# Holding MLP units behind attention matmuls in TensorE's order, and pinning the additions of narrow inputs on VectorE

## The chip, the cores and the metric

The kernel runs on one core of one Trainium2 chip. The metric is device time in microseconds (us). Three runs of the kernel before took 1078.59, 1073.54 and 1074.20 us; their median is 1074.2 us. Its profile is of one further execution.

## The reference

Attention over a batch of 4, with 8 heads, 576 positions and a head size of 64, and then two MLPs (512 to 2048 to 512) over all 2304 tokens, one behind the other, all in float32.

```python
scores = scale * np.matmul(q, k.transpose(0, 1, 3, 2))      # (4, 8, 576, 576), scale = 1/8
scores = np.where(causal, -1000000000.0, scores)
a = np.exp(scores - scores.max(-1, keepdims=True))
a /= a.sum(-1, keepdims=True) + 1e-09
local = np.matmul(a, v)
mem_ret = np.einsum('bhsd,bhde->bhse', q_p, M_prev)         # q_p = phi(q), elementwise: elu(q) + 1
mem_norm = np.einsum('bhsd,bhd->bhs', q_p, z_prev)[..., None] + 1e-06
attn_out = g * mem_ret / mem_norm + (1 - g) * local         # g = sigmoid(beta), one number per head

x = attn_out.transpose(0, 2, 1, 3).reshape(2304, 512)
x = elu(x @ moe_w_in) @ moe_w_out                           # first MLP
x = leaky(x @ moe2_w_in) @ moe2_w_out                       # second MLP, leaky(h) = max(0.01 h, h)
```

## The kernel before

**Numbers.** A float32 matrix product is made of products of two halves: each operand is a high part (a rounded copy) and a low part (what the rounding left). xh and xl are the halves of an MLP input, gh and gl those of an activation, dh and dl, ah and al, qph and qpl those of attention's operands. The high part is a copy on ScalarE or VectorE, the low part a subtraction on VectorE or GpSimd. The MLP's three matmuls for each 128 x 128 block of weights are high x high, low weight x high, and high weight x low (`h_mm`, `o_mm`).

**Attention.** A tile is one batch element (`tiles1`, 0 to 3), and in it four pairs of heads are done one after the other. For each head and group of rows there is an item with three stages: its scores (`score`, one or two spans of keys for each block of rows; the score matmuls, lines 428 and 429, go to one of three PSUM banks sc; VectorE reduces them, line 431; ScalarE exponentiates, line 436), its transposes (`t0`, `t1`, `t1b`, `t1c`: GpSimd scales the rows, line 451, TensorE transposes them to a bank tp, line 457, and ScalarE and VectorE split the result into halves, lines 249 and 250), and its products with v and the memory (`pv`, line 524, to the only bank po; VectorE copies po to xp, line 531, which a DMA writes to DRAM). A new pair of heads also needs its keys and queries transposed (lines 294, 339), their halves made (kk, kl, qs; lines 302 and 343), and phi of the queries (lines 330 and 250, qph and qpl, by way of po). `weave` mixes the stages of three items that follow each other.

**MLP units beside attention.** When a tile's attention is done, its 576 tokens go through a part of the first MLP (7 of its 16 blocks of 128 hidden columns) while the next tile's attention runs. `phase1_units` makes the list: for each half of the tile (288 tokens, a narrow input) it loads what attention wrote, adds the two heads' parts (`u_x`, the four additions of line 682, one for each 128 columns, on VectorE; tile 0 has none), splits the sum (`split_x`: line 610 on ScalarE, line 614 on GpSimd), and then come 7 units of 12 matmuls of the first layer (`u_h`, line 621) and 4 units of 21 of the second (`u_o`, line 649). Of tiles 1 to 3 each half's input is read by four DMAs (lines 675 and 676) into x and y, of which there is one buffer each.

**What sets the order.** The loop at lines 762 to 780 goes through attention's units with a planned cost in ns for each. pos is the cost up to here. Once pos has passed the point at which a unit of the MLP may start (its tile's end plus DELAY), each attention unit earns credit, and a unit whose cost is covered is written into the program there. A scheduler then makes each engine's order: it keeps what depends on what, takes what its own timing believes to be ready, and among that goes by priority, by and large the place in the program. `tc.high_priority(offset=FILL_OFF)` lets an MLP unit count as 20 instructions earlier. `tc.keep_in_program_order(add)` forbids that an instruction be moved on its engine past those written around it; before, it stands on the first of each four additions only. On the chip each engine runs its order as it stands and waits at semaphores.

When attention is over, the units left (mostly of tile 3) are merged with the loading of further weights, and the two MLPs' wide stages follow, in which TensorE has a matmul at all times.

Of the kernel before, what the change touches and what calls it, by code (L numbers as in the profile page):

```python
# [19 lines left out]
def _f(ap):  # L20
    return ap.bitcast(F32)
# [3 lines left out]
def kernel(  # L25
# [14 lines left out]
    nc = tc.nc  # L40
# [10 lines left out]
    SHIFT = {"prep": 0.0, "score": -0.3, "tr": 0.0, "pv": -0.1}  # L51
    V32 = 1
    FILL_OFF = 20
    LEAD = 0.4
    PC = 200
    HC = 1.0
# [84 lines left out]
    tiles1 = [(b, 0, 5) for b in range(B)]  # L141
# [64 lines left out]
    def bank(tag):  # L206
        return psum.tile([P, 512], F32, tag=tag, bufs=BANKS[tag], name=tag)
# [31 lines left out]
    def copy(eng, dst, src):  # L239
        if eng == "A":  # L240
            nc.scalar.copy(dst, src)  # L241
        else:
            (nc.vector if eng == "V" else nc.gpsimd).tensor_copy(dst, src)  # L243
# [357 lines left out]
    def mtile(tag, bufs, dt=F32, shape=None):  # L601
        shape = shape or (NW,)
        pool = pools.get(("own", tag), pools["mlp"])
        return pool.tile([P] + list(shape), dt, tag=tag, bufs=bufs, name=tag)

    def split_x(xt, w, par):
        xh = mtile(f"xh{par}", 1, F32R, (NKC, NW))[:, :, 0:w]
        xl = mtile(f"xl{par}", 1, F32R, (NKC, NW))[:, :, 0:w]
        for c in range(NKC):
            hi = nc.scalar.copy(xh[:, c], xt[:, c])  # L610
            if c == 0 and not tail:
                tc.keep_in_program_order(hi)
            pools["cast", par] = hi.ins
            nc.gpsimd.tensor_tensor(out=xl[:, c], in0=xt[:, c], in1=_f(xh[:, c]), op=ALU.subtract)
        return xh, xl

    def h_mm(ph, wi, xh, xl):
        n_mm = 0
        for kc in range(NKC):
            for wj, xx in ((0, xh), (1, xh), (0, xl)):  # L620
                nc.tensor.matmul(ph, wi[:, wj, kc, :], xx[:, kc, :], start=n_mm == 0, stop=n_mm == 11)  # L621
                n_mm += 1
# [8 lines left out]
    def elu(ph, w):  # L631
        e = mtile("e", EB)[:, 0:w]
        nc.scalar.activation(out=e, in_=ph, func=AF.Relu, scale=-1.0)
        nc.scalar.activation(out=e, in_=e, func=AF.Exp, scale=-1.0)
        nc.vector.scalar_tensor_tensor(out=e, in0=e, scalar=-1.0, in1=ph, op0=ALU.add, op1=ALU.max)
        return g_split(e, w)
# [7 lines left out]
    def o_mm(py, fs, key, ec, gs, first, last, opens=True, closes=True):  # L644
        for f in fs:
            wo = wo_tiles[key, f]
            gh, gl = gs[f]
            for n_mm, (wj, gg) in enumerate(((0, gh), (1, gh), (0, gl))):
                nc.tensor.matmul(  # L649
                    py, wo[:, wj, ec * P:(ec + 1) * P], gg,  # L650
                    start=opens and f == first and n_mm == 0, stop=closes and f == last and n_mm == 2,
                )
# [5 lines left out]
    def h_bank():  # L658
        nonlocal n_ph
        n_ph += 1  # L660
        return bank("tp" if tail and n_ph % 2 else "pm")

    def phase1_units(ti):

        mine = [(pi, o, w, {}) for pi, (pt, o, w, _) in enumerate(parts) if pt == ti]

        def u_load(pi, o, w, st):
            xt = st["t"] = mtile("x", 1, F32, (NKC, NW))[:, :, 0:w]
            if ti < V32:
                nc.sync.dma_start(xt, xm_scr[ti][:, :, o:o + w])  # L670
                return
            x2 = st["t2"] = mtile("y", 1, F32, (NKC, NW))[:, :, 0:w]
            for j in range(2):
                ps, pz = slice(64 * j, 64 * j + 64), slice(64 - 64 * j, 128 - 64 * j)
                nc.sync.dma_start(xt[ps], xq_scr[ti][j][ps, :, o:o + w])
                nc.sync.dma_start(x2[ps], xq_scr[ti][j][pz, :, o:o + w])

        def u_x(pi, o, w, st):
            xt = st["t"]
            if ti >= V32:  # L680
                for c in range(NKC):
                    add = nc.vector.tensor_tensor(out=xt[:, c], in0=xt[:, c], in1=st["t2"][:, c], op=ALU.add)
                    if c == 0:
                        tc.keep_in_program_order(add)
            st["x"] = split_x(xt, w, pi % 2)
            for n in range(2):
                nc.sync.dma_start(xp_scr[n][pi], _f(st["x"][n]))
            st["g"] = {}

        units = [(0, lambda: u_x(*mine[0]))]  # L690
        for k, (pi, o, w, st) in enumerate(mine):

            def u_h(f, w=w, st=st):
                ph = h_bank()[:, 0:w]
                h_mm(ph, wi_tiles[0, f], *st["x"])
                st["g"][f] = elu(ph, w)

            def u_o(ec, pi=pi, w=w, st=st):
                py = bank("sc" if tail else "pm")[:, 0:w]
                o_mm(py, range(NFA), 0, ec, st["g"], 0, NFA - 1)  # L700
                y = mtile("st", 2)[:, 0:w]
                copy(E_Y, y, py)
                nc.sync.dma_start(y_scr[pi][:, ec], y)

            for f in range(NFA):
                units.append((HC * 12 * w / 2.4, lambda f=f, u=u_h: u(f)))
                if k + 1 < len(mine) and f == 1:
                    units.append((0, lambda k=k: u_load(*mine[k + 1])))
                if k + 1 < len(mine) and f == NFA - (4 if ti == len(tiles1) - 1 else 2):
                    units.append((0, lambda k=k: u_x(*mine[k + 1])))  # L710
            for ec in range(NKC):
                units.append((3 * NFA * w / 2.4, lambda ec=ec, u=u_o: u(ec)))
        return lambda: u_load(*mine[0]), units

    def merge(a, bu):
# [4 lines left out]
        while ia < len(a) or ib < len(bu):  # L720
            if ib >= len(bu) or (ia < len(a) and fa / ta <= fb / tb + LEAD):
                c, u = a[ia]
# [8 lines left out]
    def close_decode():  # L731
        wst_a.__exit__(None, None, None)
        pools["decode_bank"] = None
        pools["outer"] = tc.tile_pool(name="mlpx", bufs=1, reuse_waits="tile", side="left")
        early = pools["outer"].__enter__()
        for tag in ("x", "y", "xh0", "xl0"):
            pools["own", tag] = early
        pools["own"] = tc.tile_pool(name="mlp", bufs=1, reuse_waits="tile", side="left")
        pools["mlp"] = pools["own"].__enter__()
# [19 lines left out]
    dec = [lambda f=f: load_w(0, wpa, w1i, w1o, f, f) for f in range(NFA)]  # L759
    fill = []  # L760
    credit = pos = 0.0
    for c, u, done in att:
        u()
        pos += c
        while dec and pos >= c0 * DSPAN * (NFA - len(dec)) / NFA:
            with tc.high_priority(offset=0):
                dec.pop(0)()
        if done == 0:
            close_decode()
        if done is not None:  # L770
            fetch, more = phase1_units(done)
            fetch()
            fill += [(pos + DELAY, c2, u2) for c2, u2 in more]
        if fill and fill[0][0] <= pos:
            credit += c * rate
        while fill and fill[0][0] <= pos and fill[0][1] <= credit:
            _, c2, u2 = fill.pop(0)
            credit -= c2
            with tc.high_priority(offset=FILL_OFF):
                u2()  # L780
    side = [(c, u) for _, c, u in fill]
    del pools["cast", 0]
# [117 lines left out]
    for gi, (t0, w) in enumerate(wide):  # L900
        pos = {}
# [61 lines left out]
```

## Time and profile before

| what | value |
|---|---|
| runs | 1078.59, 1073.54, 1074.20 us; median 1074.2 us |
| the profiled execution | 1075.3 us, of which the span of instructions is 1073.5 us |
| TensorE busy | 1042.7 us, 97% of the span |
| VectorE, ScalarE, GpSimd busy | 595.5, 483.5, 532.4 us |
| granted TensorE clock, mean | 0.995 of 2.4 GHz |

The three other engines have most of their work in the first 400 us, beside attention; from there on they wait for TensorE. Times in rows of the trace count from the span's start. PE is TensorE, DVE VectorE, ACT ScalarE, POOL GpSimd. A matmul's own time overlaps the next one's, so what TensorE loses is read from the idle time in square brackets, with what ended it behind the arrow, and not from the times of single matmuls.

### The profile page before, as it was taken

What the parts mean: (1) busy time and instruction counts of PE and PEld (TensorE: products, weight loads), DVE (VectorE), ACT (ScalarE), POOL (GpSimd) and SP (SyncE); (2) the same over time, 40 slices, a digit from 0 to 9 for tenths busy, and PEclk for the clock granted to TensorE, in tenths of its full rate; (3) what the DMA queues carried; (4) which work ended last, traced back from release to release, by engine and by line L of the source; (5) the groups of instructions that cost most, each with busy time, mean ns of one, the idle gap of its engine ahead of it and who ended that gap; (6) DMA issues with size and microseconds to landing.
All of it is one profiled execution on the core that took longest, in us unless ns stands there. A gap on an engine that the chain in (4) does not pass through costs nothing.

```text
span 1073.5 us, 17323 instructions
## 1 busy us (share of the span) xinstructions
PE 1042.7 (97%) x5904; PEld 911.4 (85%) x5904; DVE 595.5 (55%) x1382; ACT 483.5 (45%) x1169; POOL 532.4 (50%) x674
## 2 busy tenths in 40 slices
PE   7998899999998999999999999999999999999997
PEld 4776799989998998988888889888888888888896
DVE  6889987788879748576762325654322221232232
ACT  6999887778877635544442224332211211110111
POOL 7675775667657626654543225855422422222221
PEclk9999999999999999999999999999999999999999
DMA  7754544564446238765562304430200100000010
GB/s 183 197 144 116 162 137 105 124 169 144 108 121 164 89 95 286 251 227 188 191 224 66 118 1 138 157 118 1 79 1 1 64 15 1 10 30 1 1 40 20
DMA packets 150408, 115.05 MB, mean 107 GB/s; under 512 B 80048, under 2 KB 142000, under 8 KB 150320
## 3 DMA queue, kind: packets, MB, share of 16 engines
q1 hardware_dynamic: 150320, 113.94, 35.6%
q8 instruction: 47, 0.77, 0.3%
q14 instruction: 41, 0.34, 0.1%
HBM read 78.52 MB, written 31.85 MB: 103 GB/s over the span
## 4 chain that ended last, share of the span: by engine, by line
PE 87%; DVE 6%; DMA 3%; issue 1%; ACT 1%; SPq 1%; POOL 0%; DVEq 0%; ACTq 0%; POOLq 0%
PE pm L621 20%; PE tp L621 16%; PE sc L911 14%; PE sc L649 10%; PE pm L649 4%; PE po L911 4%; PE po L524 4%; PE tp L457 4%; PE po L649 3%; PE pm L524 2%; PE sc L428 1%; PE sc L426 1%; PE sc L429 1%; DVE pt L431 1%; DMA y<-xq 1%
## 5 line engine op out<-in xcount | busy, mean ns | idle before, releaser
L628 POOL TENSOR_TENSOR gl<-e,gh 128x512 fp32r<-128x512 f32 (+2 forms) x181 | 202.8, 1123 | 378.0 <-DVE gh L243 266.4
L621 PE MATMUL tp<-xw,w 128*128 128x512 f32 (+1 forms) x504 | 144.0, 367 | 0.0
L621 PE MATMUL pm<-xw,w 128*128 128x512 f32 (+1 forms) x496 | 142.1, 369 | 0.0
L911 PE MATMUL sc<-w,gh 128*128 128x512 f32 x448 | 135.9, 390 | 0.0
L451 POOL TENSOR_SCALAR pt<-pt,rs,omg 128x128 f32<-128x128 f32 (+4 forms) x160 | 102.5, 649 | 22.9 <-DVE rs L446 18.2
L649 PE MATMUL sc<-gh,w 128*128 128x512 f32 (+2 forms) x438 | 105.4, 340 | 0.3 <-DVE gh L243 0.3
L621 PEld LDWEIGHTS tp<-xw,w 128*128 128x128 f32 x504 | 91.8, 189 | 16.1
L621 PEld LDWEIGHTS pm<-xw,w 128*128 128x128 f32 x496 | 90.6, 188 | 16.1
L436 ACT ACTIVATE pt<-pt,mx 128x128 f32<-128x128 f32 (+4 forms) x160 | 93.0, 583 | 16.6 <-DVE mx L431 15.7
L911 PEld LDWEIGHTS sc<-w,gh 128*128 128x128 f32 x448 | 83.1, 188 | 16.5
L621 PE MATMUL tp<-xv,w 128*128 128x512 f32 (+1 forms) x252 | 92.5, 367 | 0.0
L621 PE MATMUL pm<-xv,w 128*128 128x512 f32 (+1 forms) x248 | 91.4, 369 | 0.0
L640 ACT ACTIVATE e<-pm 128x512 f32<-128x512 f32 (+1 forms) x40 | 22.2, 554 | 145.2 <-PE pm L621 142.2
L138 POOL TENSOR_TENSOR w<-wm,w 128x512 fp32r<-128x512 f32 x50 | 65.8, 1337 | 37.9 <-ACT w L241 37.9
L641 DVE TENSOR_TENSOR e<-tp,e 128x512 f32<-128x512 f32 (+1 forms) x40 | 25.5, 636 | 106.2 <-ACT e L640 106.2
L911 PE MATMUL sc<-w,gl 128*128 128x512 f32 x224 | 84.3, 389 | 0.0
L243 DVE CAST gh<-e 128x512 fp32r<-128x512 f32 (+2 forms) x146 | 75.4, 520 | 13.8 <-PE po L911 3.1
L649 PEld LDWEIGHTS sc<-gh,w 128*128 128x128 f32 x438 | 74.9, 188 | 9.3 <-DVE gh L243 0.6
L621 PE MATMUL pm<-xh,w 128*128 128x288 f32 x368 | 81.3, 308 | 1.5 <-ACT xh L610 1.4
L457 PE MATMUL tp<-ident,pt 128*128 128x128 f32 x480 | 80.3, 276 | 2.3 <-ACT ah L247 0.8
L641 DVE TENSOR_TENSOR e<-pm,e 128x512 f32<-128x512 f32 (+1 forms) x40 | 25.4, 636 | 102.4 <-ACT e L640 102.4
L640 ACT ACTIVATE e<-tp 128x512 f32<-128x512 f32 (+1 forms) x40 | 22.1, 552 | 117.2 <-PE tp L621 117.2
(157 smaller groups left out, 2444.7 us busy)
## 6 DMA issues: line engine op xcount, KB each, us to landing
wraw<-in_moe_w_in_dram SPq DMA_DIRECT2D x32, 512.0 KB, 3.9
wraw<-in_moe_w_out_dram SPq DMA_DIRECT2D x32, 512.0 KB, 4.7
xh<-xh SPq DMA_DIRECT2D x8, 576.0 KB, 3.1
xl<-xl SPq DMA_DIRECT2D x8, 576.0 KB, 4.1
ys<-st SPq DMA_DIRECT2D x32, 144.0 KB, 2.8
x<-x1s SPq DMA_DIRECT2D x9, 512.0 KB, 3.8
out_dram<-st SPq DMA_DIRECT2D x36, 128.0 KB, 1.7
vn<-in_v_dram SPq DMA_DIRECT2D x64, 64.0 KB, 2.3
```

Of the source, the lines that this page charges most:

```text
L138: nc.gpsimd.tensor_tensor(out=w[:, 1, a], in0=t[:, a], in1=_f(w)[:, 0, a], op=ALU.subtract)
L243: (nc.vector if eng == "V" else nc.gpsimd).tensor_copy(dst, src)
L436: nc.scalar.activation(out=pt[0:m, 0:nk], in_=pt[0:m, 0:nk], func=AF.Exp, scale=-1.0, bias=mx[0:m, last:last + 1], accum_out=self.pd["ss"] ...
L451: nc.gpsimd.tensor_scalar(out=pt, in0=pt, scalar1=rs[0:m, i:i + 1], scalar2=omg[0:m, h:h + 1], op0=ALU.mult, op1=ALU.mult,)
L457: nc.tensor.transpose(dst, self.p[c][:, k0:k0 + kn], ident)
L524: nc.tensor.matmul(po[:, a:b], w, x, start=i == 0, stop=i == len(mms) - 1)
L621: nc.tensor.matmul(ph, wi[:, wj, kc, :], xx[:, kc, :], start=n_mm == 0, stop=n_mm == 11)
L628: nc.gpsimd.tensor_tensor(out=gl, in0=g, in1=_f(gh), op=ALU.subtract)
L640: nc.scalar.mul(t, ph, 0.01)
L641: nc.vector.tensor_tensor(out=t, in0=ph, in1=t, op=ALU.max)
L649: nc.tensor.matmul(py, wo[:, wj, ec * P:(ec + 1) * P], gg, start=opens and f == first and n_mm == 0, stop=closes and f == last and n_mm == 2,)
L911: nc.tensor.matmul(pos[tb], gg[:, tb * P:(tb + 1) * P], wo[:, wj, :], start=f == 0 and n_mm == 0, stop=f == NF - 1 and n_mm == 2,)
```

## The change

Two edits. In `u_x`, every addition of a tile but the last is kept in program order, not only the first of four. In the loop, each attention unit with a cost leaves a mark: the planned position behind it and the last matmul that it traced. Each MLP unit is then traced under `tc.issue_after(hold)`, where hold is the last mark that lies at least SLACK = 4000 planned ns back. That adds an edge, for the order only, from that attention matmul to each instruction of the unit on the same engine, TensorE: in TensorE's order none of the unit's matmuls may stand ahead of it. No wait at run time is added by the edge, no instruction is added or removed, and the other engines' instructions are held by nothing but their data.

```diff
     FILL_OFF = 20
+    SLACK = 4000.0
     LEAD = 0.4
...
                     add = nc.vector.tensor_tensor(out=xt[:, c], in0=xt[:, c], in1=st["t2"][:, c], op=ALU.add)
-                    if c == 0:
+                    if c == 0 or ti < len(tiles1) - 1:
                         tc.keep_in_program_order(add)
...
     credit = pos = 0.0
+    marks = []
+    traced = nc.cur_bb.bb.instructions
+
+    def last_matmul():
+        return next(i for i in reversed(traced) if i.engine == mybir.EngineType.PE)
+
     for c, u, done in att:
         u()
         pos += c
+        if c:
+            marks.append((pos, last_matmul()))
...
             credit -= c2
-            with tc.high_priority(offset=FILL_OFF):
+            hold = next(m for p, m in reversed(marks) if p <= pos - SLACK)
+            with tc.issue_after(hold), tc.high_priority(offset=FILL_OFF):
                 u2()
```

Ten lines are added, so a line of the kernel before stands 1 line further on in most of the changed file (L682 is L683, L621 is L622) and 10 further on behind the loop. TensorE has 935 matmuls of the MLP ahead of its last attention matmul before, and 909 now. The first difference in its order lies at the matmul that starts at 173 us of the trace, the last at 568 us.

TensorE, tile 1, where its second pair of heads is about to begin (kk_3162 and qs_3230 are keys and queries of a head, pt_ are rows of exponentiated scores, gh and gl activations of the MLP). Before:

```order
L524 MATMUL po<-dl_155,vv 128x128
L457 MATMUL tp<-ident,pt_168 128x128
L457 MATMUL tp<-ident,pt_3387 128x128
L428 MATMUL sc<-kk_3162,qs_3230 128x288
L429 MATMUL sc<-kl_1_178,qs_3230 128x288
L457 MATMUL tp<-ident,pt_3394 128x128
```

Now:

```order
L650 MATMUL pm<-gl,w_793 128x288
L429 MATMUL sc<-kk_3162,qs_3230 128x288
L430 MATMUL sc<-kl_1_178,qs_3230 128x288
L650 MATMUL pm<-gh,w_905 128x288 x2
L650 MATMUL pm<-gl,w_905 128x288
L650 MATMUL pm<-gh,w_1010 128x288 x2
L650 MATMUL pm<-gl,w_1010 128x288
L458 MATMUL tp<-ident,pt_3394 128x128
```

The last matmuls of the second layer of tile 0's second half have moved in between attention's: before, the last of them stood 24 rows above the first row shown, and no unit followed until the next tile's input was there.

VectorE, the same place some instructions later (x<-x,y are the additions of the first half of tile 1; qpl, qs_3652 and dl are what the next matmuls of attention need). Before, three of the four additions stand 57 rows further up, and the fourth here:

```order
L431 ISA pt_3585,mx<-sc,mask,mx 128x288
L431 ISA mx 128x1
L682 TENSOR_TENSOR x<-x,y 128x288
L343 TENSOR_TENSOR qs_3652<-sc,qs_3652 64x256
L250 TENSOR_TENSOR dl_147<-tp,dh_145 128x384
```

Now:

```order
L432 ISA pt_3585,mx<-sc,mask,mx 128x288
L432 ISA mx 128x1
L683 TENSOR_TENSOR x<-x,y 128x288 x3
L251 TENSOR_TENSOR ac<-tp,ac 64x320
L683 TENSOR_TENSOR x<-x,y 128x288
L251 TENSOR_TENSOR qpl<-po,qph 128x320
L344 TENSOR_TENSOR qs_3652<-sc,qs_3652 64x256
```

All four additions stand together, ahead of qpl and qs_3652.

VectorE, the additions of the second half of tile 2. Before:

```order
L635 SCALAR_TENSOR_TENSOR e<-e,pm 128x288
L302 TENSOR_TENSOR kl_1_176<-sc,kk_5753 64x256
L682 TENSOR_TENSOR x<-x,y 128x288 x3
L531 COPY xp<-po 128x256
L250 TENSOR_TENSOR dl_155<-tp,dh_153 128x384
```

Now:

```order
L388 SCALAR_TENSOR_TENSOR ph_f<-qn,ph_e 128x640
L447 RECIPROCAL rs<-rs 128x2
L636 SCALAR_TENSOR_TENSOR e<-e,pm 128x288
L683 TENSOR_TENSOR x<-x,y 128x288 x4
L432 ISA pt_5997,mx<-sc,mask,mx 128x288
```

They have moved seven score spans down, and what follows them is the reduction of a score instead of the copy that frees the only bank po.

## Rows read from the trace of the kernel before

**Rows 1.** The page, busy time of each engine (us, share of the span, instructions)
```profile
PE 1042.7 (97%) x5904; PEld 911.4 (85%) x5904; DVE 595.5 (55%) x1382; ACT 483.5 (45%) x1169; POOL 532.4 (50%) x674
```
**Rows 2.** Windows: stretch, length, busy of each engine, clock, DMA share, GB/s
```profile
172.00:394.00 222.00, 214.50 (x1633) 209.81 (x1631) 179.34 (x534) 166.79 (x474) 143.37 (x224) 0.98 0.47 125
394.00:426.00 32.00, 29.69 (x219) 28.93 (x218) 20.62 (x32) 15.07 (x31) 15.68 (x17) 1.00 0.88 282
426.00:1073.50 647.50, 641.60 (x3101) 543.31 (x3099) 250.24 (x389) 160.80 (x273) 254.44 (x219) 1.00 0.24 80
```
**Rows 3.** Waits of PE, 172 to 425 us: total us, times, longest
```profile
PE pm L621 <- ACT xh L610: 1.4, 1, 1.4
PE tp L621 <- DVE e L635: 0.6, 1, 0.6
...
PE tp L457 <- DVE dl L250: 0.4, 2, 0.2
PE sc L649 <- DVE gh L243: 0.3, 1, 0.3
```
**Rows 4.** Timeline of PE: start, us, instruction, [idle before <- what ended it]
```profile
202.47 0.33 PE L428 MATMUL sc<-kk,qs 128*128 128x128 f32 x1 [0.72 <-DVE qs L343]
...
220.19 0.40 PE L428 MATMUL sc<-kk,qs 128*128 128x288 f32 x1 [0.77 <-DVE mx L431]
...
223.81 0.33 PE L428 MATMUL sc<-kk,qs 128*128 128x128 f32 x1 [0.83 <-DVE qs L343]
...
225.44 0.39 PE L524 MATMUL po<-qph,ms 128*128 128x256 f32 x1 [0.43 <-DVE qpl L250]
...
307.75 0.39 PE L428 MATMUL sc<-kk,qs 128*128 128x256 f32 x1 [0.68 <-DVE mx L431]
...
323.21 0.33 PE L428 MATMUL sc<-kk,qs 128*128 128x128 f32 x1 [0.62 <-DVE qs L343]
...
325.86 0.52 PE L330 MATMUL po<-ident,ph_e 128*128 128x128 f32 x3 [0.87 <-DVE qpl L250]
...
344.31 0.41 PE L524 MATMUL po<-qph,ms 128*128 128x320 f32 x1 [1.92 <-DVE xp L531]
```
**Rows 5.** Windows behind two of the idles; the clock is the third number from the right
```profile
226.00:230.00 4.00, 4.00 (x21) 4.00 (x20) 3.87 (x10) 2.02 (x7) 3.19 (x4) 0.57 0.84 321
...
344.00:350.00 6.00, 5.69 (x32) 5.66 (x33) 5.81 (x17) 4.43 (x12) 3.44 (x6) 0.72 0.26 77
```
**Rows 6.** Line 682: count, duration in ns (shortest, middle, longest), first and last start
```profile
L682 DVE TENSOR_TENSOR x<-x,y x24: 445/456/3086, 200.7 to 421.2; 128x288 f32<-128x288 f32 x24
```
**Rows 7.** Timeline of DVE at three groups of additions
```profile
200.68 1.20 DVE L682 TENSOR_TENSOR x<-x,y 128x288 f32<-128x288 f32 x3 [2.02 <-DMA y<-xq]
...
303.36 1.20 DVE L682 TENSOR_TENSOR x<-x,y 128x288 f32<-128x288 f32 x3 [1.38 <-DMA vn<-in_v_dram]
...
339.80 4.12 DVE L682 TENSOR_TENSOR x<-x,y 128x288 f32<-128x288 f32 x3 [1.24 <-DMA xq<-xp]
343.85 0.41 DVE L531 COPY xp<-po 128x256 f32<-128x256 f32 x1
344.18 0.54 DVE L250 TENSOR_TENSOR dl<-tp,dh 128x384 fp32r<-128x384 f32 x1
```
**Rows 8.** Timeline of POOL beside the last of these groups
```profile
341.31 0.80 POOL L628 TENSOR_TENSOR gl<-e,gh 128x288 fp32r<-128x288 f32 x1
342.07 1.53 POOL L614 TENSOR_TENSOR xl<-x,xh 128x288 fp32r<-128x288 f32 x2
```
**Rows 9.** Windows with attention alone on PE (two), and with MLP alone
```profile
214.40:226.60 12.20, 9.85 (x71) 8.22 (x70) 11.38 (x36) 10.93 (x33) 7.65 (x15) 0.99 0.43 113
...
319.30:326.10 6.80, 5.22 (x40) 4.51 (x39) 6.55 (x19) 5.70 (x17) 4.48 (x8) 1.00 0.56 146
...
394.40:404.10 9.70, 9.70 (x75) 9.70 (x75) 2.82 (x6) 1.87 (x5) 2.10 (x4) 1.00 0.69 191
```

## The prediction

> **What bounds the kernel now.** I read the page's busy times first. TensorE is busy for 1042.7 of 1073.5 us [rows 1], so a change can gain only where it idles or runs slowly. The windows by stage [rows 2] say where. After 426 us it is busy for 641.6 of 647.5 us, at full clock; what it idles there lies at the very end, out of reach of an order that is the same from the 568th us on. In 172 to 394 us, attention with MLP units woven in, 7.5 us are missing, and between 394 and 426 us, where attention has ended, 2.3 us. Up to 172 us TensorE's order is unchanged, so what is lost before that stays lost.
>
> The waits [rows 3, 4] name each of these idles. Behind attention they are 0.72 and 0.15 us at 202 us; 0.77, 0.83, 0.24 and 0.43 us between 220 and 226 us; 0.68 us at 307 us; 0.62 and 0.87 us at 323 and 326 us; 1.92 us at 344 us. (The 0.15 and the 0.24 us are the two waits for dl of [rows 3].) That is 7.2 us. After attention come 1.38, 0.32 and 0.61 us, 2.3 us. All of attention's waits are for VectorE. To this the clock is added: from 226 to 230 us, right behind the waits of 220 to 226 us, the granted share is 0.57, and from 344 to 350 us, behind the 1.92 us, 0.72 [rows 5]; TensorE fell from 2.4 to 1.2 GHz each time. It was busy for all or nearly all of both, so this is lost work: 4 x 0.43 = 1.7 us and 6 x 0.28 = 1.7 us. In all 9.5 + 3.4 = 12.9 us can be had, and not more.
>
> Two causes stand behind the waits. The first is the additions of line 682 on VectorE. Three of each four stand early in its order and wait there for their data: 2.02, 1.38 and 1.24 us at 200, 303 and 339 us [rows 7], and the third at 339 us takes 3.09 us where the middle one of 24 takes 0.46 [rows 6], while GpSimd works on without a pause until 343.6 us [rows 8]. The idles at 202, 307 and 344 us follow, each for something that VectorE has behind those additions; the 1.92 us is for the copy at 343.85 us. The second cause is stretches in which TensorE has attention alone. From 214.4 to 226.6 us (68 matmuls in the order) it is busy for 9.85 of 12.2 us, from 319.3 to 326.1 us (39 matmuls) for 5.22 of 6.8 us [rows 9], VectorE being busy for 11.38 and 6.55 us of these. No other run of attention matmuls behind 172 us idles except for the additions; the next longest has 25.
>
> **The pinning.** Now the additions of tiles 1 and 2 stay where the program writes them. In VectorE's order they move back to the need of them: by 12 and 3 score spans in tile 1, by 12 and 7 in tile 2, for the first three of each four. The two first halves need no wait any more, since earlier instructions on VectorE have already waited as far; the second halves wait for DMAs that have had several us more. So the stalls in front of the additions go: at TensorE 0.72 + 0.15 + 0.68 + 1.92 = 3.5 us and, with the last of them, 1.7 us of clock. I take 5.2 us; at least the 0.9 us at 202 us (the plainest case), at most 5.2.
>
> What is late next: the additions now stand as a block in front of other work. In tile 1 these are the subtraction qpl and the copies qs, for which TensorE waits at 223.81 and 225.44 us already [rows 4]; in tile 2 qs, dl and the copy xp. Three additions more, 1.20 us by the first row of [rows 7], stand there each time. In tile 2 I count the 1.2 us whole. Bounds: nothing, if TensorE has enough else to do, and 1.2 + 2.6 = 3.8 us, if one addition waits as the one at 340.84 us did (3.09 - 0.46). At the second halves nothing that TensorE needs at once stands behind the block but a score's reduction, with three PSUM banks between them: 0 us, at most 2.6 us.
>
> The Trainium skill (SBUF — State Buffer, "SBUF: two separate sides") says that a VectorE instruction with two SBUF inputs and a GpSimd instruction that reads SBUF exclude each other, and that the loser waits for the whole instruction of the winner. By that rule a block behind one GpSimd instruction (0.80 us in [rows 8]) would cost 0.8 us; this case's row has 2.6 us across several of them, so the row decides and the upper end above stays.
>
> **The hold.** The units' matmuls can't go ahead of an attention matmul that stands 4000 of the planner's units back. Before, they ran out at 214 us: there was nothing left to put between attention matmuls until 226 us. Now 21 matmuls of the second linear layer lie in that stretch, and another 21 in tile 2's. They take 0.13 us each (9.70 us for 75 from 394.4 to 404.1 us [rows 9]), 2.7 us each time, in which VectorE catches up. The longest runs of attention alone become 38, 38, 35 and 31 matmuls instead of 68 and 39.
> - Tile 2's stretch: its 0.62 + 0.87 = 1.5 us go; between 0 and 1.5.
> - Tile 1's stretch: the units help, the block of additions hurts. By the order TensorE reaches the matmul that waits for qpl with 8 transposes behind its last score, 1.1 us at the 9.85 / 71 = 0.14 us of [rows 9]. VectorE has then a reduction, the block with a subtraction between, and qpl to do: 4 x 0.40 us and three times about 0.5 us, as the subtraction at 344.18 us [rows 7], 3.1 us. That is a wait of about 2.0 us, where 2.3 us were lost. I take no change, with the clock's 1.7 us still lost. Bounds: 4.0 us gained (2.3 + 1.7) and 2.6 us lost.
> - The four runs that remain: 1.0 us together. Bounds: 0, since runs up to 25 idle nowhere, and 4 x 1.5 = 6.0 us, as the run of 39 did.
>
> **After attention.** 909 MLP matmuls stand ahead of the last attention matmul, where 935 stood: 26 x 0.13 = 3.4 us of work move behind it. The work is the same in all, and it covers more of the way of the last attention output through DRAM. Before, the second narrow half of tile 3 came 1.38 us late; with 3.4 us more work ahead it is there. The other 0.93 us wait for gh and e and may stay; I take 1.5 us gained, between 0 and 2.3.
>
> **Sum.** -5.2 - 1.5 + 0 - 1.5 + 1.2 + 1.0 = -6.0 us. The profiled execution took 1075.3 us, 1073.5 of span and 1.8 around it, so 1069.3 us; it was 1.1 us above the median of 1074.2, so I predict 1068.2 us.
>
> **Rivals.**
> *The block takes the stalls' place* (chance 0.20). Four additions in a row meet GpSimd's work, their own low halves included, and at both first halves one waits as at 340.84 us. For it: 24 additions, of which one alone cost 2.6 us. Against: it needs GpSimd without a pause, and that is one in 24. -5.2 - 1.5 - 1.5 + 3.8 + 2.6 + 1.0 = -0.8 us, 1073.4 us. The skill's exclusion rule, cited above, is the mechanism of this one.
> *The hold starves TensorE* (0.10): slower. A held unit can't fill a wait of attention that comes early, and all four remaining runs idle like the run of 39, 1.5 us each, three of them drawing the lower clock for 1.7 us. It decides if a run above 30 matmuls behaves like 39 rather than like 25. Then there are 6.0 + 5.1 us instead of 1.0; tile 2's block costs 1.2, and nothing is gained at tile 2's stretch or after attention: -5.2 + 1.2 + 11.1 = +7.1 us, 1081.3 us. Against: the first idle in the run of 39 came 3.9 us in (323.2 against 319.3), and the new runs, 31 to 38 matmuls at 5.22 / 40 = 0.13 us, are 4.0 to 4.9 us long: they get that far only at their ends.
> *Tile 1's stretch goes too* (0.15): the 21 matmuls put VectorE so far ahead that qpl is ready. -6.0 - 4.0 = -10 us, 1064.2 us.
> That the hold does nothing can be left out: the order differs from the 173rd us on.
>
> **How the numbers follow.** The forecast has 0.55, with a range of its own of 1065 to 1072 us. About 0.5%, 5.4 us, is what a measurement can tell from no change here; the line is at 1068.8 us. The forecast lies on both sides of it, 0.35 faster and 0.20 the same. With the third rival faster has 0.50; with the first the same has 0.40; slower has 0.10. The range reaches from 1063 us, where most of the third rival is in, to 1076 us, above the first; it leaves out the second.
>
> **What would show it.** Right: no idle of TensorE over 0.5 us at the places of 202, 307 and 344 us; no wait of an addition on VectorE for a DMA but in tile 3; no clock of 0.72 near 344 us; one wait for qpl of 2 to 2.5 us at tile 1's change of head pair; attention's end 5 to 9 us earlier. Wrong: several idles over 1 us in the runs of 31 to 38, or three clock drops behind 172 us instead of two; additions of 2 us and more in front of qpl or qs; or idles gone from attention and found again between 394 and 430 us.

## The result, and the profile after

The changed kernel takes 1084.7 us, the median of 5 runs (1084.0 to 1085.0); in the same session the kernel before took 1074.2 us (1073.3 to 1078.6). The ratio is 1.0089, with a 95% interval of 1.0072 to 1.0106. It is slower by some 10 us where 6 us less were forecast, and it lies outside the stated range of 1063 to 1076 us. The profiled execution took 1084.9 us with a span of 1083.2 us.

First the line of busy times on the page of the changed kernel, which answers to [rows 1]:

```profile
PE 1047.1 (97%) x5904; PEld 912.8 (84%) x5904; DVE 595.9 (55%) x1382; ACT 483.4 (45%) x1169; POOL 529.6 (49%) x674
```

The matmuls are the same 5904, yet TensorE is busy for 4.4 us longer: the loss is not in long waits alone. The windows by stage answer to [rows 2]. Line numbers up to the loop over attention are those of before plus 1.

```profile
172.00:394.00 222.00, 208.72 (x1573) 199.96 (x1573) 180.76 (x526) 163.62 (x469) 140.79 (x221) 0.99 0.46 122
394.00:426.00 32.00, 32.00 (x244) 32.00 (x243) 16.23 (x32) 14.97 (x34) 13.21 (x15) 1.00 0.79 240
426.00:1083.00 657.00, 649.92 (x3160) 551.26 (x3159) 255.90 (x402) 166.45 (x283) 257.31 (x224) 1.00 0.25 83
```

In the stage that the change was to help, 13.3 us are missing instead of 7.5. Behind attention TensorE is indeed covered (32.00 of 32), but attention's last matmul ends at 402.0 us instead of 394.4.

This first profile was late already at 172 us, where no order has changed: the same matmul, the third of a group of transposes, starts at 174.3 us, against 171.1 us before. The change did not do it: in a second profile of the changed kernel it starts at 171.2 us, in one of the kernel before at 171.8. What differs from one execution to the next is, for one thing, where TensorE falls from 2.4 to 1.2 GHz in that stretch. Each such time loses some 1.7 us (in the first profile of before, 4 x 0.31 + 4 x 0.11 from 20 to 28 us, where the granted shares are 0.69 and 0.89), and the first profile of the changed kernel had three ahead of 172 us where that of before had one. The clock is not the whole of it, since the second profile of the changed kernel had two and is 0.1 us behind. The kernel before has them elsewhere in its second profile as well. The second profile of the changed kernel (span 1082.0 us) therefore serves for the comparison. Its waits of TensorE between 172 and 440 us, all of them, answer to [rows 3]:

```profile
PE po L525 <- DVE qpl L251: 3.2, 2, 2.6
PE tp L458 <- DVE ac L251: 2.2, 1, 2.2
PE po L525 <- DVE xp L532: 1.5, 2, 1.1
PE pm L622 <- ACT xh L611: 1.4, 1, 1.4
PE tp L458 <- DVE dl L251: 1.0, 3, 0.4
PE pm L622 <- POOL xl L615: 0.9, 1, 0.9
PE sc L429 <- issue: 0.9, 1, 0.9
PE sc L340 <- DVE mx L432: 0.6, 1, 0.6
PE sc L429 <- DVE mx L432: 0.6, 1, 0.6
PE sc L650 <- POOL gl L629: 0.5, 1, 0.5
PE tp L458 <- DVE al L251: 0.2, 1, 0.2
```

They add up to 13.0 us, where the idles of before made 9.5. The old waits for qs at 202 and 307 us and for xp at 344 us are gone; new are ac at 206 us, a longer one for qpl at 230 us, xp at 263 us, and xh with one before it at 337 us (times of the first profile; in the second they come 1 to 3 us earlier). Right behind those at 206, 230 and 337 us the granted clock falls from 2.4 to 1.2 GHz. These are three windows of the second profile, each with some time at either level:

```profile
204.00:212.00 8.00, 6.38 (x37) 6.33 (x38) 6.50 (x17) 1.54 (x6) 2.45 (x5) 0.79 0.39 98
228.00:240.00 12.00, 9.40 (x51) 9.19 (x51) 8.29 (x22) 6.15 (x18) 8.22 (x11) 0.72 0.79 209
340.00:344.00 4.00, 4.00 (x21) 4.00 (x20) 2.97 (x11) 2.23 (x7) 2.09 (x5) 0.58 0.87 254
```

8 x 0.21 + 12 x 0.28 + 4 x 0.42 = 6.7 us of clock are gone behind 172 us, where before lost 3.4. The idle part of the first two windows is the wait that comes ahead of the lower clock. Waits and clock together are 3.5 + 3.3 = 6.8 us more than before.

The wait for ac at 206 us is the one that nothing in the prediction leads to. The rows of the first profile around it, DVE, GpSimd (POOL) and TensorE together (start, duration, and in brackets the idle time before it and its releaser):

```profile
204.50 2.11 POOL L452 TENSOR_SCALAR pt<-pt,rs,omg 64x320 f32<-64x320 f32 x3 [0.31 <-DVE rs L447]
205.28 2.77 DVE L388 SCALAR_TENSOR_TENSOR ph_f<-qn,ph_e 128x640 f32<-128x640 f32 x1
206.58 0.78 POOL L629 TENSOR_TENSOR gl<-e,gh 128x288 fp32r<-128x288 f32 x1
208.09 0.48 DVE L251 TENSOR_TENSOR ac<-tp,ac 64x320 fp32r<-64x320 f32 x1
208.72 0.52 PE L458 MATMUL tp<-ident,pt 128*128 128x128 f32 x3 [2.25 <-DVE ac L251]
```

The product ph_f of line 388 reads two operands from SBUF and normally takes 0.82 us. Here it takes 2.77: GpSimd works without a pause from 204.50 to 207.36 us (a chain, in what follows), and ph_f ends 0.69 us behind it. The subtraction ac stands behind ph_f on VectorE, and TensorE waits for ac. In the kernel before, the same ph_f stands behind ac and meets a pause of GpSimd:

```profile
207.34 0.82 DVE L387 SCALAR_TENSOR_TENSOR ph_f<-qn,ph_e 128x640 f32<-128x640 f32 x1
208.25 0.22 POOL L445 TENSOR_SCALAR rs<-ss 128x2 f32<-128x2 f32 x1 [1.78 <-DVE ph_f L387]
```

### The profile page after: what moved, and what is told of

Same layout as the page of the kernel before. It is cut to its first block, busy times and chain, and to the rows that moved or that the text cites. A ratio compares the mean times of both kernels' runs of the same rounds, so it can differ in the third digit from the quotient of the medians.

```text
span 1083.2 us, 17328 instructions
## 1 busy us (share of the span) xinstructions
PE 1047.1 (97%) x5904; PEld 912.8 (84%) x5904; DVE 595.9 (55%) x1382; ACT 483.4 (45%) x1169; POOL 529.6 (49%) x674
## 4 chain that ended last, share of the span: by engine, by line
PE 83%; DVE 6%; DMA 4%; POOL 2%; issue 2%; ACT 2%; SPq 1%; DVEq 0%; POOLq 0%; ACTq 0%
PE pm L622 19%; PE tp L622 15%; PE sc L921 14%; PE sc L650 9%; PE po L921 4%; PE pm L650 4%; PE tp L458 3%; PE po L525 3%; PE po L650 3%; PE pm L525 2%; PE sc L427 2%; PE sc L429 1%; PE sc L430 1%; DVE pt L432 1%; SPq L215 1%
## 5 line engine op out<-in xcount | busy, mean ns | idle before, releaser
L629 POOL TENSOR_TENSOR gl<-e,gh 128x512 fp32r<-128x512 f32 (+2 forms) x181 | 200.0, 1107 | 381.2 <-DVE gh L244 273.0
L622 PE MATMUL tp<-xw,w 128*128 128x512 f32 (+1 forms) x504 | 144.1, 367 | 0.0
L622 PE MATMUL pm<-xw,w 128*128 128x512 f32 (+1 forms) x496 | 141.7, 369 | 0.0
L622 PEld LDWEIGHTS tp<-xw,w 128*128 128x128 f32 x504 | 91.9, 189 | 16.2
L622 PEld LDWEIGHTS pm<-xw,w 128*128 128x128 f32 x496 | 90.6, 188 | 16.1
L622 PE MATMUL tp<-xv,w 128*128 128x512 f32 (+1 forms) x252 | 92.5, 367 | 0.0
L622 PE MATMUL pm<-xv,w 128*128 128x512 f32 (+1 forms) x248 | 91.4, 368 | 0.0
L458 PE MATMUL tp<-ident,pt 128*128 128x128 f32 x480 | 84.2, 280 | 6.2 <-DVE ac L251 2.2
L622 PE MATMUL pm<-xh,w 128*128 128x288 f32 x368 | 80.2, 304 | 1.6 <-ACT xh L611 1.4
L432 DVE CUSTOM_DVE_ANT_0 pt<-sc,mask 128x128 f32<-128x128 f32 (+4 forms) x160 | 69.5, 444 | 11.6 <-PE sc L430 6.1
```

The lines of the kernel that those rows point to most:

```text
L432: nc.vector.tensor_tensor_reduce(out=pt[0:m, k0:k0 + n], in0=sc[0:m, 0:n], in1=mk, op0=ALU.add, op1=ALU.min, scale=-0.125, scalar=mx[0:m, ...
L458: nc.tensor.transpose(dst, self.p[c][:, k0:k0 + kn], ident)
L629: nc.gpsimd.tensor_tensor(out=gl, in0=g, in1=_f(gh), op=ALU.subtract)
```

## The experiments

Theory C: the hold lets the planner draw VectorE's instructions that work from SBUF to SBUF onto chains of GpSimd; each stands still there, and TensorE waits for what is queued behind it. Theory S: the held units leave attention without cover, whatever VectorE does. Theory N: the block of additions does it.

**Both kernels once more, and each half of the change alone.** The pinning alone drops `tc.issue_after(hold)`; the hold alone keeps the old condition:

```
e1_pin                                             e1_hold
-  with tc.issue_after(hold), tc.high_priority(..) -  if c == 0 or ti < len(tiles1) - 1:
+  with tc.high_priority(offset=FILL_OFF):         +  if c == 0:
```

> The kernel before, profiled once more. Theory P (the 3.1 us that the changed kernel loses ahead of 172 us, in an order that is the same, come from where the stretches at the lower clock happen to fall in an execution): this second profile has its stretches of 3.4 us at other times than 21.5, 226.3 and 345.8 us, and TensorE reaches the 172 us mark up to 3 us earlier or later than in the first. Rival Q (the place of the stretches is a property of the program): they fall within 1 us of the same times, and the mark too.

> The changed kernel once more, on the same chip as the next two. Theory P: stretches at other times than 29.6, 104.7, 125.2 and 340.2 us, the time between 1081 and 1085 us. Rival Q: the same times within 1 us, 1084 to 1085 us. In both TensorE's waits behind 172 us stand where they stood: 2.2 us for the copy ac at 206 us, 2.6 us for qpl at 230 us, about 1 us at 263 us and 2.4 us at 337 us.

> The pinning alone, without the hold. Theory H (the hold brings the new waits at 206 and 230 us, the pinning takes the old ones at 202, 307 and 344 us): 1068 to 1072 us, no idle of over 0.5 us at 202, 307 and 344 us, the idles at 220 to 226 and 319 to 326 us as before. Rival N (the block of additions brings the new waits): 1078 to 1084 us, with waits for qpl, qs and xh behind it.

> The hold alone, the additions pinned as before (the first of each four). Theory H: 1081 to 1086 us, the waits at 206 and 230 us as in the changed kernel, and the old ones for the additions about 340 us again. Rival N: 1070 to 1075 us, without the 2.2 us at 206 us and the 2.6 us at 230 us.

Each time below is a median, and in brackets behind it stand the ratio to the kernel before, run beside it, and its 95% interval. The ratio is not formed from the medians and can differ from theirs by 0.1%.

Measured: before 1078.2 us, one run, its lower clock at 100, 120 and 420 us; changed 1084.6 us (1.0082, 1.0066 to 1.0099), lower clock at 100, 120, 204, 228 and 340 us. So the times at the lower clock ahead of 172 us change from one execution to the next, as P had it, and the waits of over 1 us behind it return within 0.1 us. The pinning alone took 1073.6 us (0.9978, 0.9966 to 0.9990), the hold alone 1098.7 us (1.0231, 1.0209 to 1.0252). The hold is what costs: 11.0 us on top of the pinning, 24 us without it. H's 1068 to 1072 us for the pinning was too low, and its 1081 to 1086 us for the hold alone far too low. N, with 1078 to 1084 us for the pinning, is out as the main cause. The waits of the pinning alone from 172 to 440 us add up to 7.4 us:

```profile
PE sc L650 <- DVE gh L244: 2.6, 1, 2.6
PE pm L622 <- ACT xh L611: 1.6, 1, 1.6
PE tp L458 <- DVE al L251: 1.1, 1, 1.1
PE sc L340 <- DVE kl L303: 0.8, 1, 0.8
PE sc L429 <- DVE mx L432: 0.8, 2, 0.6
PE sc L429 <- DVE qs L344: 0.3, 1, 0.3
PE pm L622 <- DVE e L636: 0.2, 1, 0.2
```

The longest of them, for gh at 418 us, is not the pinning's own: the kernel before has 2.6 us of it in its second profile and 0.3 in its first.

In the hold alone the same ph_f meets a chain of seven instructions of GpSimd, and takes 5 us:

```profile
203.84 2.10 POOL L452 TENSOR_SCALAR pt<-pt,rs,omg 64x320 f32<-64x320 f32 x3 [2.45 <-DVE rs L447]
204.62 5.01 DVE L388 SCALAR_TENSOR_TENSOR ph_f<-qn,ph_e 128x640 f32<-128x640 f32 x1
205.91 2.28 POOL L615 TENSOR_TENSOR xl<-x,xh 128x288 fp32r<-128x288 f32 x3
208.16 0.79 POOL L629 TENSOR_TENSOR gl<-e,gh 128x288 fp32r<-128x288 f32 x1
210.29 0.87 PE L458 MATMUL tp<-ident,pt 128*128 128x128 f32 x3 [5.51 <-DVE ac L251]
```

The chain ends at 208.95 us and ph_f at 209.63, 0.68 us later, as in the changed kernel: it does not run slowly, it stands until the chain is about over and then takes its own time. It is not so at every chain. In the same profile, 32 us on, a ph_f gets in behind the first of three multiplications, and it is GpSimd that takes longer (2.75 us for the three instead of 2.10):

```profile
236.63 2.75 POOL L452 TENSOR_SCALAR pt<-pt,rs,omg 64x320 f32<-64x320 f32 x3 [0.67 <-DVE rs L447]
236.81 1.33 DVE L388 SCALAR_TENSOR_TENSOR ph_f<-qn,ph_e 128x640 f32<-128x640 f32 x1
```

So I counted the ph_f, additions and copies vv behind 172 us that took over 0.25 us longer than by themselves. Through more than one instruction of GpSimd stood 4 of 11 in the changed kernel's first profile, 2 of 13 in the hold alone, none of 12 in the pinning alone, and one of 8 before. What decides whether one gets in is not shown.

**GpSimd's multiplications made narrow, and a milder hold.** In the first three, instructions are replaced after the planner has set the order, so all orders stay word for word:

```
for GpSimd multiplications of line 452 (numbers 87 to 89, from 0, or all 160), behind the planner:
-  pt[:, 0:320], pt[:, 0:448], pt[:, 0:576], ...
+  pt[:, 0:32]            # same name, order, waits and signals
e2_slack8000:
-    SLACK = 4000.0
+    SLACK = 8000.0
```

> The changed kernel, every engine's order unchanged; GpSimd's three multiplications of line 452 at 204.5 to 206.6 us work on 32 columns instead of 320, 448 and 576 (so part of one item's scaling is left out). Theory C (the hold moves VectorE's instructions with two SBUF inputs onto stretches of GpSimd without a pause, and TensorE waits for what stands behind them): the product ph_f of line 388 takes 0.8 to 0.9 us instead of 2.77, TensorE's wait for ac at 206 us goes from 2.2 to under 0.4 us, and the kernel is 1.5 to 4 us faster than the changed one (1080.6 to 1083 us). Rival S (the held units leave attention without cover, so the next wait takes the place of this one): the wait moves to another instruction within 10 us, and the time stays within 1 us of 1084.6.

> The changed kernel, every engine's order unchanged; all 160 multiplications of line 452 on GpSimd work on 32 columns (most of the scaling of the scores is left out), so GpSimd has some 80 us less to do in attention. To be compared with the next kernel. Theory C: the lead of the pinning alone over the changed kernel, 11 us, shrinks to 5 us or less. Rival S: it stays at 9 us or more, since VectorE's and ScalarE's work and TensorE's order are the same.

> The pinning alone without the hold, with the same 160 multiplications of line 452 on 32 columns, every engine's order as in the pinning alone. Theory C: 1066 to 1072 us, less than 5 us ahead of the changed kernel with the same cut. Rival S: 9 us or more ahead of it.

> The changed kernel with a milder hold: the units stand behind an attention matmul 8000 instead of 4000 of the planner's units back. 12000 and more give the order of the pinning alone, so this lies between the pinning (1073.6 us) and the changed kernel (1084.6 us) in its order. Theory S (the more hold, the less cover): between the two, 1075 to 1083 us. Theory C (what counts is which of VectorE's instructions meet GpSimd): anything from 1071 to 1086 us, as its waits for what stands behind lengthened VectorE instructions come out; without such ones 1071 to 1075 us.

Measured: three multiplications narrow, 1081.1 us (1.0060, 1.0046 to 1.0074), 3.5 us less in the medians and 2.4 by the ratios. ph_f takes 0.89 us, the wait at 206 us falls to 0.3 us, and none over 0.7 us came in its place:

```profile
202.41 0.89 DVE L388 SCALAR_TENSOR_TENSOR ph_f<-qn,ph_e 128x640 f32<-128x640 f32 x1
PE tp L458 <- DVE ac L251: 0.3, 1, 0.3
```

All narrow: the changed kernel 1073.5 us (0.9987, 0.9977 to 0.9998), the pinning alone 1070.4 us (0.9958, 0.9939 to 0.9976). So the width of these multiplications costs the changed kernel 11.1 us and the pinning alone 3.2, and the lead of the pinning shrinks from 11.0 to 3.1 us, as C said. No VectorE instruction of the three kinds stands through more than one of GpSimd any more. GpSimd's busy time fell by 42 us, not the 80 expected. Of the changed kernel's 11.1 us, 4.3 are listed waits (13.0 against 8.7 us), and the mean granted clock of the runs, 0.992 against 0.996, makes some 4 us more as an estimate; the rest was not traced. The milder hold took 1077.3 us (1.0025, 1.0011 to 1.0039), between the two, which both theories allow; its longest wait, 2.1 us at 356 us, stands behind four additions of 1.0 to 1.8 us.

**Pauses in GpSimd's chain, and narrow additions.** The first three leave nothing out:

```
for each element-wise GpSimd instruction, behind the planner:
+  nc.gpsimd.drain()      # placed right behind it
e3_narrow_add: the 24 additions of line 683
-  x[:, c, 0:288] + y[:, c, 0:288]
+  x[:, c, 0:32] + y[:, c, 0:32]
```

> The changed kernel with a drain instruction behind each of GpSimd's 603 element-wise instructions; nothing is left out, and every engine's order is otherwise the same. Theory C (an instruction of VectorE with two SBUF inputs stands still until GpSimd's chain of instructions without a pause has ended, and then takes its own time: 208.05 - 207.36 = 0.69 us behind the chain at 206 us): the drain makes a pause behind each, so ph_f at 205 us takes under 1.8 us instead of 2.77, TensorE's wait for ac is under 1.3 us, and the kernel takes 1076 to 1082 us. Rival G (the pause is too short to let VectorE in, or GpSimd pays more for the drains than VectorE gains): 1084 us or more, ph_f unchanged.

> The pinning alone with the same drains. Theory C: 1069 to 1073.5 us, since the same kernel with narrow multiplications on GpSimd took 1070.4; no VectorE instruction with two SBUF inputs over 1.3 us longer than its median. Rival G: 1074 us or more.

> The hold alone with the same drains. Theory C: the waits of 5.5 us at 205 us and of 2.2 us at 266 us, both behind a lengthened ph_f (5.01 and 2.99 us), go to under 2 and under 1 us; 1086 to 1094 us instead of 1098.7. Rival G: 1098 us or more. Rival S (no cover): the waits move elsewhere, 1096 us or more.

> The changed kernel, orders unchanged; the 24 additions of line 683 work on 32 columns instead of 288 (most of the addition is left out). Theory B (the block of additions is what TensorE waits for at 229.9 us): four additions of 0.40 us become some 0.1 us each, so the 2.6 us wait for qpl falls to 1.2 to 1.6 us, and the 1.4 us wait for xh at 338 us by 1 us or more (one addition took 1.75 us there); 1080 to 1082.5 us. Rival S: the wait for qpl stays over 2 us, since its input or ScalarE's copy is late as well; 1083.5 to 1085 us.

Measured: 1102.2 us (1.0242, 1.0222 to 1.0262) with the hold and the pinning, 1096.6 (1.0192, 1.0170 to 1.0213) with the pinning, 1105.8 (1.0278, 1.0257 to 1.0299) with the hold. Both sides were half right. C's times were all missed, by 12 to 23 us: a drain leaves GpSimd idle for 0.16 to 0.19 us, which is dearer in all than what VectorE gains (rival G). But ph_f at 208 us took 0.83 us in the changed kernel and TensorE waited no more for ac, as C had it (0.71 and 0.58 us there are now for GpSimd's pt), and the three kernels drew together: hold and pinning stand 5.6 us behind the pinning instead of 11.0, the hold alone 9.2 instead of 25.1. The drawing together speaks for C only in part, since the drains also bring new waits for pt in all three (4.6 us in the changed kernel). In the three profiles 25 instructions of the three kinds are lengthened behind 172 us, and none stands through more than one of GpSimd's. The narrow additions took 1082.2 us (1.0057, 1.0041 to 1.0073), 2.4 us less: the wait for qpl fell from 2.60 to 1.53 us, which is four times 0.45 - 0.18 us, and the wait for xh from 1.4 to 1.2, not by the 1 us or more expected.

```profile
229.12 0.35 PE L525 MATMUL po<-qph,ms 128*128 128x256 f32 x1 [1.53 <-DVE qpl L251]
```

Theory B holds for 1.1 us at its first place, and it is a small part of the loss.

**Two drains, both cuts, and a version that the profiles point to.**

```
e4_two_drains: drains only behind multiplications 87 and 88, from 0 (at 204.5 us)
e4_narrow_both, e4_pin_narrow_both: all of line 452 and all of line 683 on 32 columns
e4_pin_gh: the pinning alone, and
-    attending = False          # ahead of the planner's merge of the narrow units
     merge(side, ...)
+    attending = False          # until here gh is copied by ScalarE
```

> The changed kernel with two drains on GpSimd alone, behind the first two of the three multiplications at 204.5 us; nothing left out, all orders the same. Theory C: ph_f gets in at the first pause, so it takes under 1.6 us instead of 2.77 and the kernel gains most of what narrowing those three gave (3.5 us): 1081 to 1083 us, at the price of 0.4 us of GpSimd. Rival (the 3.5 us came from the GpSimd work that was left out, not from the blocked instruction): 1084 to 1085 us.

> The changed kernel, orders the same, with both the 160 multiplications of line 452 and the 24 additions of line 683 on 32 columns (both left out for the most part). If GpSimd's chains and the block of additions are the whole of the loss against the pinning alone, this is within 1.5 us of the next kernel: 1069 to 1072 us. If the hold also starves TensorE by itself, it stays 3 us or more behind the next.

> The pinning alone with the same two cuts, orders as in the pinning alone: 1067 to 1070.5 us, within 1.5 us of the kernel before in this list if the two causes are the whole, 3 us or more ahead of it if not.

> The pinning alone, and the copies gh of the narrow units stay on ScalarE until the last narrow unit instead of going to VectorE when attention ends (the line that sets this moves behind the merge). In the pinning alone TensorE waits 2.57 us for a gh at 418 us, whose copy stands behind four additions that take 4.35 us against GpSimd. With the copy on ScalarE that wait goes: 1068.5 to 1072 us, faster than the kernel before by 3 us or more. Rival: ScalarE's own queue (decoding of weights, 1.1 us pieces) delays gh as much, or another wait at the change of stages takes its place: 1073 to 1075 us.

Measured: two drains 1082.9 us (1.0086, 1.0067 to 1.0104), 1.7 us less than the changed kernel in the medians and inside what C expected; by the ratios (1.0086 against 1.0082) no gain can be told. What the drains do is plain in the rows of VectorE and GpSimd:

```profile
201.90 0.60 POOL L452 TENSOR_SCALAR pt<-pt,rs,omg 64x320 f32<-64x320 f32 x1 [0.31 <-DVE rs L447]
202.68 0.83 DVE L388 SCALAR_TENSOR_TENSOR ph_f<-qn,ph_e 128x640 f32<-128x640 f32 x1
202.69 1.40 POOL L452 TENSOR_SCALAR pt<-pt,rs,omg 128x448 f32<-128x448 f32 x1 [0.19 <-issue]
203.53 0.48 DVE L251 TENSOR_TENSOR ac<-tp,ac 64x320 fp32r<-64x320 f32 x1
```

Now ph_f comes within GpSimd's pause, is first by 0.01 us and takes its 0.83 us, and it is GpSimd's multiplication that stands: 1.40 us instead of 0.71. TensorE waits 0.30 and 0.58 us for pt there, which fits that two drains give less than narrow multiplications. So this run does not settle whether the 3.5 us came from the blocked ph_f alone or in part from the work left out.

Both cuts: the changed kernel 1070.7 us (0.9967, 0.9955 to 0.9979), the pinning 1063.9 (0.9905, 0.9887 to 0.9923). The lead is 6.8 us, not the 1.5 that chains and block as the whole cause would leave. So the hold costs something that neither cut takes away, as theory S has it; its mechanism was not tested. The two causes don't add: narrow additions are worth 2.9 us to the changed kernel and 6.5 to the pinning once the multiplications are narrow, for in the pinning the waits for gh (2.6 us) and al (1.1 us) go with them. The two profiles are 6.0 us apart. Of these, 2.8 are waits (7.5 against 4.7 us from 172 to 440 us), with 1.5 us for qpl the longest. The lower clock takes 3.4 us of each, and gaps under 0.3 us are few (1.1 against 0.6 us). The rest is time in which TensorE counts as busy, 1041.6 against 1038.1 us for the same matmuls. What makes it longer was not tried.

The pinning with gh on ScalarE took 1071.7 us (0.9967, 0.9952 to 0.9983), the fastest median of those that compute everything: 2.8 us ahead of the kernel before in the medians and 3.5 by the ratio, where 3 or more were expected. Against the pinning alone (0.9978, 0.9966 to 0.9990) no gain can be told. The wait for gh fell from 2.6 to 1.6 us and is now ScalarE's, so the rival was right for the rest.

## Why the prediction was wrong, by its steps

- *The pinning, -5.2 + 1.2 = -4.0 us.* Right in kind, too large in size. By itself the pinning gives 0.22% (0.10 to 0.34%), 1 to 3.7 us. The idles at 202, 307 and 344 us are gone, and the block of additions is late at a next place, though for xh and not for qs, dl or xp: 1.6 us at 322 us.
- *The hold at the longest runs, "1.0 us together" for the four that remain.* This is the step that failed, with *After attention* in its wake. It took the length of a run of attention matmuls as what decides, and put new waits in shorter runs at nothing ("runs up to 25 idle nowhere"). In the second profile the four long runs idle 0.42 us together, after the 32nd matmul of one of them, so that term was rather too large. But the 2.2 us for ac come with no attention matmul behind the last MLP one, and those of 2.6 (tile 1's, which had a term), 1.1, 0.9 and 1.4 us after 19, 6, 15 and 18. In these rows it counts which VectorE instruction stands in front of the one that TensorE waits for, and what GpSimd does then; with the multiplications narrow, 11.1 us of the time go. A part of the hold's cost stays open, as the two cuts together show. The hold measured +11.0 us where its terms (-1.5, 0, +1.0, -1.5) made -2.0.
- *The exclusion was priced for the additions alone* ("one in 24"). The trace of before had it elsewhere: ph_f from 0.80 to 1.40 us, and the copy vv of line 243 from 0.34 to 1.53 us, there without a wait of TensorE behind them:

```profile
L387 DVE SCALAR_TENSOR_TENSOR ph_f<-qn,ph_e x16: 798/825/1398, 9.3 to 358.5; 128x640 f32<-128x640 f32 x16
L243 DVE CAST vv<-vn x24: 337/364/1527, 79.2 to 348.6; 128x320 fp32r<-128x320 f32 x24
```

- *Tile 1's stretch, a wait of "about 2.0 us" for qpl.* Right in place, and 2.60 us long; 1.07 of them are shown to be the additions' width.
- *Tile 2's stretch, -1.5 us.* Its 0.62 and 0.87 us went, but 0.94 and 1.44 us stand at 336 to 338 us instead, where VectorE has a ph_f of 1.88 us and an addition of 1.75 in its queue.
- *After attention, -1.5 us.* From 394 to 426 us all 2.3 us were gained and 1.4 of them lost again by 434 us (0.5 for gl, 0.9 for xl); attention ends 6.7 to 7.6 us later, not 5 to 9 earlier.
- *The clock.* One lower stretch fewer was forecast. The second profile has three places behind 172 us, 6.7 us in all, 3.3 more than before.

The rival *The hold starves TensorE* (0.10) named the side and nearly the size, 1081.3 us, with three clock drops as its sign. Its mechanism, runs above 30 matmuls that idle, is not what the trace shows.

For the blocking the rows say more than the rule weighed in the prediction. By the Trainium skill (SBUF — State Buffer, "Who interferes with whom") a VectorE instruction with two SBUF inputs and a GpSimd instruction that reads SBUF contend, and whichever issues first holds the other off for its whole instruction. By that rule ph_f waits for one GpSimd instruction, at most 0.8 us by an estimate from the rows of the hold alone (0.82 us is the longest there). The 1.33 us at 237 us agree; the 5.01 us at 205 us do not, with 4.2 us of waiting across six instructions.

## What to carry to other kernels

A change that only moves cover must be weighed at every wait that it uncovers, not at the longest bare stretch: look through the trace for instructions that take far longer than their median, and ask what the new order queues behind them. Here those on VectorE were ones that work from SBUF to SBUF, and beside a GpSimd that never pauses one of them took 5.01 us instead of 0.82. Test such a cause by making the other engine's instructions narrow behind the planner, with the order unchanged.

## What was not expected of the hardware

- A VectorE instruction with two SBUF inputs can stand through several of GpSimd's instructions, to the end of its chain: the ph_f of 2.77, 5.01, 2.99 (hold alone, 265 us) and 1.88 us each ended 0.68 or 0.69 us behind the chain's end. More often it gets in after one, and GpSimd's next one stands in turn. With a drain behind each of GpSimd's instructions, none of the 25 counted stood through more than one.
- Copies with one SBUF input suffer too: vv (line 244) took up to 2.28 us against 0.37 in the changed kernel. The subtraction ac, with one input in PSUM, did not: in the kernel before all 24 took 0.48 or 0.49 us, whether GpSimd worked beside them (204.7 us) or not (173.7 us).
